# Chunked attention and a gated feed-forward: turning the probabilities by DMA and VectorE instead of TensorE

## The chip, the cores and the metric

The kernel runs on one core of a Trainium2 chip. The metric is the device time of one execution in microseconds; the median of 3 runs of the kernel before is 509.02 us (508.95 to 509.52). Engines go by the names of the profile: PE (TensorE, the matrix products), PEld (its weight loads), DVE (VectorE), ACT (ScalarE), POOL (GpSimd), SP (SyncE, which here only issues DMA transfers). SBUF is the memory of 128 partitions that the engines work in; PSUM, in banks of 128 x 512 float32, takes PE's results.

## The reference

Inputs are q, k, v of 8 batches x 8 heads x 576 rows x 64, all float32, and the weights of the feed-forward. Attention is local to chunks of 64 rows:

```python
q_c = q.reshape(B, H, nc, chunk, D)            # chunk = 64, nc = 9; k_c, v_c alike
scores = scale * np.matmul(q_c, k_c.transpose(0, 1, 2, 4, 3))
scores = scores - np.max(scores, axis=-1, keepdims=True)
attn = np.exp(scores)
attn = attn / (np.sum(attn, axis=-1, keepdims=True) + 1e-09)
out = np.matmul(attn, v_c)
# x = out as (batch, seq, H * D = 512), then the feed-forward, d_ff = 1024:
h = np.maximum(x @ w_in, 0.0)
conv_out = sum over k in 0..2 of conv_w[k] * hp[:, k:k + S, :]   # hp: h padded by one row at both ends
gate = 1.0 / (1.0 + np.exp(-conv_out))
return (h * gate @ w_out).astype(np.float32)
```

## The kernel before

The 4608 rows (8 x 576) are 36 tiles of 128 rows, two chunks each (`t`, two chunks `s`), and 16 units of 288 rows (`u`, half a batch). Attention goes by tiles, the first product of the feed-forward by units, the second by tiles. float32 products of the feed-forward are made of three products of split operands (high and low parts, `x_h`, `x_l`, `wi_h`, `wi_l`, `g_h`, `g_l`, `wo_h`, `wo_l`).

The steps of attention for one tile, with their lines in the profile:

- `load_group`/`load_part` (L134, SP): q and k of three tiles, in pieces of 32 partitions; for tiles below 9 `load_rows` (L114). `load_v` (L146, SP): v of a tile in four DMAs, one for each chunk `s` and each half `hp` of the heads.
- `t_dve` (L163, DVE): q and k turned in blocks of 32 x 32 into `qT` and `kT`; for tiles below 9 `t_pe`/`t_copy` (L154, L158).
- `scores` (L189, PE): 16 products of 64 x 64 into half of two PSUM banks. These are the two banks of `sx`, or, from tile 12 on, also two of the six other banks, which are lent (`lent`, `give_up`) for that from then on.
- `s_max` (L199), `s_sub` (L204), both DVE and reading PSUM; `s_exp` (L209, ACT, tile `e`); `s_sum` (L213), `s_eps` (L216), `s_rec` (L219), DVE, tile `z`; `s_norm` (L222, POOL): e times 1/z.
- `p_pe` (L229, PE): four transposes of 128 x 128 by a product with the identity, into a bank; `p_copy` (L234, ACT): that bank into `pT`.
- `attn_v` (L241, PE): 16 products into half of two banks; `x_hi` (L271, ACT) and `x_lo` (L275, DVE) split the result into `x_h` and `x_l`.

From tile 12 on two tiles go together: one step `both` runs `attn_v` of the last pair and then `scores` of the next pair on PE. A lent bank pair was two tiles of one bank each, so that `s_max` and `s_sub` of a tile that stands there are two instructions (128 x 256 each); on `sx` they are one (128 x 512).

The feed-forward: `mm1` (L284, PE, 12 products of 128 x 290 for each unit and each eighth `f` of d_ff), `h_relu` (L290), `c_mid` (L295), `c_left` (L299), `c_right` (L305), `c_sig` (L311), `c_mul` (L314, which frees the bank), `g_hi` (L324, ACT), `g_lo` (L328, POOL); `mm2` (L337, PE, 3 products of 128 x 512 for each tile and `f`), `o_copy` (L342, ACT), `o_store` (L345, SP). At the start the weights are unpacked and split in ten pieces (L370 to L420, on ACT, DVE and POOL).

What sets the order: all of this is first written down as 2244 steps, each with an engine, a cost, what it comes after and which buffers it takes and frees. A list of numbers, `order_`, gives the order in which a planner places them; it keeps the times of engines and buffers with the steps' costs, and the kernel issues the steps in order of their planned begins. Each engine then runs its own instructions in exactly that order. Up to a planned time of 110 us PE gets warm-up products (L828, fillers) where the plan has it idle.

```python
pe_free = begin[i] + steps[i]["cost"]
steps[i]["fn"](*steps[i]["args"])
```

Buffers that matter here: `e` 3, `z` 2, `pT` 2, `v` 4, and `wt` 4 tiles of 128 x 1024 float32, used by the weights at the start and by `o_copy`/`o_store` later.

Of the kernel before, what the change touches and what calls it, by code (L numbers as in the profile page):

```python
# [30 lines left out]
def attn_ffn(ctx: ExitStack, tc: tile.TileContext, q, k, v, w_in, conv_w, w_out, out):  # L31
# [10 lines left out]
    HS = S // 2  # L42
    XU = HS + 2
# [4 lines left out]
    NU = 2 * B  # L48
# [4 lines left out]
    PAIR = 12  # L53
    scale = 1.0 / float(D) ** 0.5
# [25 lines left out]
    banks = [ps_b.tile([P, 512], F32, name=f"b{i}_ps") for i in range(6)]  # L80
# [57 lines left out]
    def load_v(st, t):  # L138

        r = rawv.tile([P, G, 2, D], F32, name="v")  # L140
        st["v"] = r
        for s in range(2):
            b, t0 = chunk(2 * t + s)
            for hp in range(2):
                j0 = 64 * (hp ^ s)
                nc.sync.dma_start(out=r[j0:j0 + C, :, s, :], in_=v[b, hp::2, t0:t0 + C, :].rearrange("g j d -> j g d"))  # L146
# [18 lines left out]
    def sx_half(i):  # L165

        cols = slice(G * C * (i % 2), G * C * (i % 2) + G * C)
        if i // 2:
            return [(slice(0, 2), sx[:, :, cols])]
        return [(slice(u, u + 1), banks[lent["y", u]].rearrange("p (u n) -> p u n", u=1)[:, :, cols]) for u in range(2)]  # L170

    def sx_bank(i, u):
        parts = sx_half(i)
        return parts[0][1][:, u, :] if len(parts) == 1 else parts[u][1][:, 0, :]
# [7 lines left out]
    def scores(st):  # L182

        qT, kT = st[0], st[1]
        for g in range(G):
            for s in range(2):
                for hp in range(2):
                    d0 = 64 * hp
                    nc.tensor.matmul(  # L189
                        sx_bank(st["s"], hp ^ s)[C * s:C * s + C, C * g:C * g + C],  # L190
# [5 lines left out]
    def s_max(st):  # L196
        st["m"] = work.tile([P, 2, G], F32, name="m")
        for us, sv in sx_half(st["s"]):
            nc.vector.tensor_reduce(out=st["m"][:, us], in_=sv.rearrange("p u (g j) -> p u g j", j=C), op=ALU.max, axis=AX.X)  # L199

    def s_sub(st):
        st["e"] = work3.tile([P, H, C], F32, name="e")
        for us, sv in sx_half(st["s"]):
            nc.vector.tensor_tensor(  # L204
                out=st["e"].rearrange("p (g u) j -> p u g j", u=2)[:, us], in0=sv.rearrange("p u (g j) -> p u g j", j=C),
                in1=st["m"][:, us].rearrange("p u (g o) -> p u g o", o=1).broadcast_to([P, us.stop - us.start, G, C]), op=ALU.subtract)

    def s_exp(st):
        nc.scalar.activation(out=st["e"], in_=st["e"], func=AF.Exp, scale=scale)  # L209

    def s_sum(st):
        st["z"] = work.tile([P, H], F32, name="z")
        nc.vector.tensor_reduce(out=st["z"], in_=st["e"], op=ALU.add, axis=AX.X)  # L213
# [4 lines left out]
    def s_rec(st):  # L218
        nc.vector.reciprocal(out=st["z"], in_=st["z"])  # L219

# [15 lines left out]
    def attn_v(st):  # L236
        for g in range(G):
            for s in range(2):
                for hp in range(2):
                    j0 = 64 * (hp ^ s)  # L240
                    nc.tensor.matmul(  # L241
                        sx_bank(st["x"], s)[D * hp:D * hp + D, C * g:C * g + C],
                        lhsT=st["v"][j0:j0 + C, g, s, :],
                        rhs=st["pT"][j0:j0 + C, g, C * s:C * s + C],
# [8 lines left out]

    def x_views(st, t, x):

        xv = [v_.rearrange("p s (g i) -> p g s i", i=C) for _, v_ in sx_half(st.get("x", 2))]
        parts = []
        for s in range(2):
            b, t0 = chunk(2 * t + s)
            for half, lo, hi in ((0, 0, HS + 2), (1, HS - 2, S)):  # L260
                i, j = max(lo, t0), min(hi, t0 + C)
                if i < j:
                    parts.append((s, i - t0, j - i, (2 * b + half) % NX, i - lo))
        if len(xv) == 1 and [p[1:4] for p in parts] == [(0, C, parts[0][3])] * 2:
            _, _, _, u, o = parts[0]
            return [(xv[0], x[:, u, :, o:o + 2 * C].rearrange("p g (s i) -> p g s i", i=C))]
        return [((xv[0][:, :, s] if len(xv) == 1 else xv[s][:, :, 0])[:, :, i:i + n], x[:, u, :, o:o + n]) for s, i, n, u, o in parts]
# [10 lines left out]
    def mm1(st, u, f):  # L278

        h_ps = banks[st["h"]]  # L280
        n = 0
        for wt, xt in ((wi_h, x_h), (wi_h, x_l), (wi_l, x_h)):
            for kt in range(KT):
                nc.tensor.matmul(  # L284
                    h_ps[:, 0:XU], lhsT=wt[:, f // 2, kt, P * (f % 2):P * (f % 2) + P], rhs=xt[:, u % NX, kt, 0:XU],
# [3 lines left out]
    def h_relu(st):  # L289
        nc.scalar.activation(out=banks[st["h"]][:, 0:XU], in_=banks[st["h"]][:, 0:XU], func=AF.Relu)  # L290

    def c_mid(st, u, f):
        st["i0"] = i0 = 2 * (u % 2)
        st["c"] = work7.tile([P, HS], F32, name="c")
        nc.scalar.mul(out=st["c"], in_=banks[st["h"]][:, i0:i0 + HS], mul=cw[:, FT + f:FT + f + 1])  # L295

    def c_left(st, u, f):
        a, i0, c = 1 - u % 2, st["i0"], st["c"]
        nc.vector.scalar_tensor_tensor(  # L299
            out=c[:, a:HS], in0=banks[st["h"]][:, i0 + a - 1:i0 + HS - 1], scalar=cw[:, f:f + 1], in1=c[:, a:HS],  # L300
            op0=ALU.mult, op1=ALU.add)
# [11 lines left out]
    def c_mul(st):  # L313
        nc.vector.scalar_tensor_tensor(  # L314
            out=st["c"], in0=st["c"], scalar=1.0, in1=banks[st["h"]][:, st["i0"]:st["i0"] + HS], op0=ALU.add, op1=ALU.mult)

    def g_views(u, f):
        g0 = HS * u % GR
        n = min(HS, GR - g0)
        return [(slice(s0, s1), slice(o, o + s1 - s0)) for s0, s1, o in ((0, n, g0), (n, HS, 0)) if s0 < s1]  # L320
# [127 lines left out]
    def split(key, t_load, src, hi=None, lo=None, lo_pool=False, half=False):  # L448
# [5 lines left out]
        if small:  # L454
# [23 lines left out]
    def att(t, key, load_key, writes):  # L478

        st = {}  # L480
        if t < NAT:
            r = "wslot" if t in W_ROWS else "slot"
            ld = step("SP", 1.25, load_key, load_rows, (st, t), take=[(r, st)], lag=3.3)
# [12 lines left out]
        ldv = step("SP", 2.65, load_key + 0.05 if t < 5 else key - 8, load_v, (st, t), [before.get("v")], take=["v"], lag=1.66)  # L496
# [21 lines left out]
        before["x"] = [(st_, t_, soft(st_, s, key + 4 * n) + [v_], w_) for n, (st_, t_, _, v_, w_, _) in enumerate(new)]  # L518
# [15 lines left out]
    def soft(st, s, key):  # L534
        s = step("DVE", 0.69, key, s_max, (st,), [s], take=["m"], bank="sx")
        s = step("DVE", 0.68, key, s_sub, (st,), [s], take=["e"], free=["m", ("sx", "s")], bank="sx")
        s = step("ACT", 0.63, key + 8, s_exp, (st,), [s])
# [5 lines left out]
        return [step("ACT", 0.59, key + 12, p_copy, (st,), [s], take=["pT"], free=[("bk", "pt")])]  # L543

# [8 lines left out]
    def group(j):  # L553
        if j not in group_loads:
# [3 lines left out]
            group_loads[j] = [step("SP", 2.05 if j % 3 != 1 else 4.0, key + 0.1 * n, load_part, (j, n % 2, n // 4, n // 2 % 2), [s], lag=1.25)  # L558
# [18 lines left out]
    until = [-(-(HS * u + HS + (0 if u % 2 else 2)) // P) for u in range(NU)]  # L577
# [285 lines left out]
```

## Time and profile before

| | |
|---|---|
| median of 3 runs | 509.02 us (508.95 to 509.52) |
| the profiled execution | 508.6 us, of which the span of the instructions is 506.8 us |
| instructions | 13087 |
| HBM read, written | 36.72 MB, 9.44 MB |
| first product of `mm1`; last product of `mm2` ends | 36.5 us; about 503.1 us |

A page row of a group reads: line, engine, operation, output<-inputs, shapes, xcount, then busy time in us, the mean ns of one, and the idle time of the engine just before them with what ended it. A row of a timeline reads: start in us, duration in us, then the same names. A row of a table by stage gives for each engine its busy time in that stage with the count of instructions, then the granted PE clock, the share of the DMA engines and GB/s. Durations of products on PE overlap, since it is pipelined; what one costs is read from start to start.

### The profile page before, as it was taken

The page shows a single profiled execution, that of the slowest core. Times are in us where ns is not written, and L with a number is a line of the kernel's source. Part 1 is how long each engine was busy: PE and PEld are TensorE (multiplying, and loading weights), DVE is VectorE, ACT ScalarE, POOL GpSimd, SP SyncE. Part 2 cuts the span into 40 slices and gives each one's busy share as a digit, 9 for nine tenths or more (in the row PEclk, how much of TensorE's full clock was granted, in tenths as well). Part 3 has the DMA queues.
Part 4 walks back from the last instruction along what each step waited for, and adds up shares of the span by engine and source line. Part 5 has one row for each costly group of instructions (what it writes and reads, how often), then busy time and mean ns, then how long its engine had stood idle before and what let it go on. Part 6 is the DMA issues. An engine that isn't in the chain of part 4 may idle for free.

```text
span 506.8 us, 13087 instructions
## 1 busy us (share of the span) xinstructions
PE 495.7 (98%) x5079; PEld 444.9 (88%) x5079; DVE 343.1 (68%) x745; ACT 312.2 (62%) x784; POOL 171.4 (34%) x237
## 2 busy tenths in 40 slices
PE   7999988999999999999999999999999999999997
PEld 7889977899888999989889999988988988998885
DVE  3889999688644787776776785767685856574300
ACT  4569986757535766666655766656665656784511
POOL 1543646425421252333240433333314143241600
PEclk9999999999999999999999999999999999999999
DMA  8987864523265453434445442334612040100111
GB/s 193 229 229 179 224 179 89 88 46 61 45 126 124 118 118 61 94 62 85 107 86 110 83 101 46 74 81 76 150 19 63 23 125 2 49 17 0 44 43 62
DMA packets 183171, 47.04 MB, mean 93 GB/s; under 512 B 175404, under 2 KB 175428, under 8 KB 183108
## 3 DMA queue, kind: packets, MB, share of 16 engines
q1 hardware_dynamic: 183108, 46.20, 40.7%
q8 instruction: 40, 0.66, 0.6%
q14 instruction: 23, 0.19, 0.1%
HBM read 36.72 MB, written 9.44 MB: 91 GB/s over the span
## 4 chain that ended last, share of the span: by engine, by line
PE 89%; DVE 5%; ACT 2%; issue 1%; DMA 1%; POOL 0%; SPq 0%; ACTq 0%
PE b_ps L337 39%; PE b_ps L284 38%; PE b_ps L229 3%; PE sx_ps L189 2%; PE sx_ps L241 2%; PE b_ps L241 1%; DMA qk<-in_moe_w_in 1%; PE b_ps L189 1%; PE b_ps L828 1%; DVE wt L379 1%; PE b_ps L154 1%; ACT wt L370 1%; DVE c L314 1%; DVE c L305 1%; DVE c L299 1%
## 5 line engine op out<-in xcount | busy, mean ns | idle before, releaser
L328 POOL TENSOR_TENSOR g_l<-c,g_h 128x288 fp32r<-128x288 f32 (+8 forms) x184 | 112.3, 633 | 204.4 <-ACT g_h L324 181.1
L337 PE MATMUL b_ps<-wo_h,g_h 128*128 128x512 f32 x288 | 116.8, 405 | 0.0
L337 PE MATMUL b_ps<-wo_h,g_l 128*128 128x512 f32 x288 | 113.6, 395 | 0.0
L337 PE MATMUL b_ps<-wo_l,g_h 128*128 128x512 f32 x288 | 113.5, 394 | 0.0
L299 DVE SCALAR_TENSOR_TENSOR c<-b_ps,cw,c 128x287 f32<-128x287 f32 (+1 forms) x128 | 65.4, 511 | 69.6 <-ACT c L295 60.9
L284 PE MATMUL b_ps<-x_h,wi_h 128*128 128x290 f32 x512 | 91.7, 301 | 1.6 <-DVE c L314 1.6
L284 PE MATMUL b_ps<-x_l,wi_h 128*128 128x290 f32 x512 | 89.6, 297 | 0.0
L284 PE MATMUL b_ps<-x_h,wi_l 128*128 128x290 f32 x512 | 89.2, 296 | 0.0
L290 ACT ACTIVATE b_ps<-b_ps 128x290 f32<-128x290 f32 x128 | 50.7, 398 | 60.0 <-PE b_ps L284 56.0
L284 PEld LDWEIGHTS b_ps<-x_h,wi_h 128*128 128x128 f32 x512 | 78.6, 189 | 9.6 <-DVE c L314 2.5
L314 DVE SCALAR_TENSOR_TENSOR c<-c,b_ps 128x288 f32<-128x288 f32 x128 | 57.0, 446 | 31.8 <-ACT c L311 30.9
L311 ACT ACTIVATE c<-c 128x288 f32<-128x288 f32 x128 | 56.3, 442 | 36.0 <-DVE c L305 35.4
L284 PEld LDWEIGHTS b_ps<-x_l,wi_h 128*128 128x128 f32 x512 | 75.9, 190 | 0.0
L284 PEld LDWEIGHTS b_ps<-x_h,wi_l 128*128 128x128 f32 x512 | 75.4, 189 | 0.0
L295 ACT ACTIVATE c<-b_ps,cw 128x288 f32<-128x288 f32 x128 | 63.7, 501 | 8.1 <-POOL g_l L328 0.8
L305 DVE SCALAR_TENSOR_TENSOR c<-b_ps,cw,c 128x288 f32<-128x288 f32 (+1 forms) x128 | 65.4, 512 | 2.7
L222 POOL TENSOR_TENSOR e<-e,z 128x512 f32<-128x512 f32 x36 | 38.5, 1073 | 84.9 <-DVE z L219 64.0
L337 PEld LDWEIGHTS b_ps<-wo_h,g_l 128*128 128x128 f32 x288 | 54.2, 188 | 12.6
L337 PEld LDWEIGHTS b_ps<-wo_h,g_h 128*128 128x128 f32 x288 | 54.4, 189 | 8.7
L324 ACT CAST g_h<-c 128x288 fp32r<-128x288 f32 (+8 forms) x184 | 58.1, 357 | 5.7 <-DVE c L314 5.0
L337 PEld LDWEIGHTS b_ps<-wo_l,g_h 128*128 128x128 f32 x288 | 54.3, 189 | 7.7
L342 ACT ACTIVATE wt<-b_ps 128x512 f32<-128x512 f32 x36 | 21.4, 596 | 25.2 <-PE b_ps L337 25.0
(59 smaller groups left out, 492.6 us busy)
## 6 DMA issues: line engine op xcount, KB each, us to landing
v<-in_v SPq DMA_DIRECT2D x144, 64.0 KB, 2.4
out<-wt SPq DMA_DIRECT2D x36, 256.0 KB, 2.3
qk<-in_q SPq DMA_DIRECT2D x96, 48.0 KB, 2.2
qk<-in_k SPq DMA_DIRECT2D x96, 48.0 KB, 2.2
qk<-in_moe_w_out SPq DMA_DIRECT2D x4, 1024.0 KB, 6.4
qk<-in_k SPq DMA_DIRECT2D x96, 24.0 KB, 1.9
qk<-in_q SPq DMA_DIRECT2D x96, 24.0 KB, 1.9
qk<-in_moe_w_in SPq DMA_DIRECT2D x4, 512.0 KB, 5.2
```

Source lines behind the costliest of these rows:

```text
L222: nc.gpsimd.tensor_tensor(out=st["e"], in0=st["e"], in1=st["z"].rearrange("p (h o) -> p h o", o=1).broadcast_to([P, H, C]), op=ALU.mult)
L284: nc.tensor.matmul(h_ps[:, 0:XU], lhsT=wt[:, f // 2, kt, P * (f % 2):P * (f % 2) + P], rhs=xt[:, u % NX, kt, 0:XU], start=n == 0, stop=n = ...
L290: nc.scalar.activation(out=banks[st["h"]][:, 0:XU], in_=banks[st["h"]][:, 0:XU], func=AF.Relu)
L295: nc.scalar.mul(out=st["c"], in_=banks[st["h"]][:, i0:i0 + HS], mul=cw[:, FT + f:FT + f + 1])
L299: nc.vector.scalar_tensor_tensor(out=c[:, a:HS], in0=banks[st["h"]][:, i0 + a - 1:i0 + HS - 1], scalar=cw[:, f:f + 1], in1=c[:, a:HS], op0 ...
L305: nc.vector.scalar_tensor_tensor(out=c[:, 0:b], in0=banks[st["h"]][:, i0 + 1:i0 + 1 + b], scalar=cw[:, 2 * FT + f:2 * FT + f + 1], in1=c[: ...
L311: nc.scalar.activation(out=st["c"], in_=st["c"], func=AF.Tanh, scale=0.5)
L314: nc.vector.scalar_tensor_tensor(out=st["c"], in0=st["c"], scalar=1.0, in1=banks[st["h"]][:, st["i0"]:st["i0"] + HS], op0=ALU.add, op1=ALU ...
L324: nc.scalar.copy(out=g_h[:, f, gs], in_=st["c"][:, cs])
L328: nc.gpsimd.tensor_tensor(out=g_l[:, f, gs], in0=st["c"][:, cs], in1=g_h[:, f, gs].bitcast(F32), op=ALU.subtract)
L337: nc.tensor.matmul(banks[st["o"]], lhsT=gt[:, f, o:o + P], rhs=wt[:, f, :], start=f == 0 and n == 0, stop=f == FT - 1 and n == 2)
L342: nc.scalar.mul(out=st["os"], in_=banks[st["o"]], mul=0.5)
```

## The change

For tiles 12 and up the probabilities are no longer transposed on PE. `s_exp` writes into one of two `wt` tiles (`of`) that both tiles of a pair share, laid out by halves `b` of the 64 keys. POOL then multiplies by 1/z twice: `s_fold` into the other `wt` tile (`to`), `s_scale` in place in `of`. `p_swap` issues four DMAs of 32 partitions that copy from `of` into `to`: for each group of 32 partitions, the half of the keys whose block belongs to the neighbouring group. `p_dve`, one instruction per tile, turns all 32 x 32 blocks of `to` into `pT`. With that the chunk, not the head half, decides the partitions of `pT`, so v of such a tile is loaded in its natural order, by one DMA (two where a batch ends), and `attn_v` and `scores` take other halves.

The lent banks become one tile `y_ps` of two banks, so `s_max` and `s_sub` are one instruction there too. Some of the planner's costs change, and `order_` is another list, for all tiles, also those below 12. The general form of the units (`UNITS`, `x_window`) gives the same units as before.

Counts over the program, from the two orders: PE transposes of probabilities 144 before, 48 now; ACT copies of them 36 and 12; POOL products with 1/z 36 and 60; DVE turns of probabilities 0 and 24; issues of v 144 and 75; issues of the swap 0 and 48; fillers 158 and 160. The counts of `mm1`, `mm2`, `scores` and `attn_v` products are the same.

The diff, cut to its core:

```diff
+    ONE_PAIR = True
+    TP = 12
...
-    banks = [ps_b.tile([P, 512], F32, name=f"b{i}_ps") for i in range(6)]
+    pair = ps_b.tile([P, 2, 512], F32, name="y_ps")
+    banks = [None] * 6
...
+        if t >= TP:
+            (b0, t0), (b1, t1) = chunk(2 * t), chunk(2 * t + 1)
+            for b, t_, p0, n in [(b0, t0, 0, P)] if b0 == b1 else [(b0, t0, 0, C), (b1, t1, C, C)]:
+                nc.sync.dma_start(out=r[p0:p0 + n].rearrange("p g u d -> p (g u) d"), in_=v[b, :, t_:t_ + n, :].rearrange("h j d -> j h d"))
+            return
...
-        if i // 2:
-            return [(slice(0, 2), sx[:, :, cols])]
-        return [(slice(u, u + 1), banks[lent["y", u]].rearrange("p (u n) -> p u n", u=1)[:, :, cols]) for u in range(2)]
+        return (sx if i // 2 else pair)[:, :, cols]
...
-                        sx_bank(st["s"], hp ^ s)[C * s:C * s + C, C * g:C * g + C],
+                        sx_bank(st["s"], hp if st["t"] >= TP + 2 else hp ^ s)[C * s:C * s + C, C * g:C * g + C],
...
     def s_exp(st):
+        if st["t"] >= TP:
+            nc.scalar.activation(out=two(st, "of").rearrange("p b h j -> p h b j"), in_=st["e"].rearrange("p h (b j) -> p h b j", b=2),
+                                 func=AF.Exp, scale=scale)
+            return
...
+    def two(st, name):
+        if name not in st["two"]:
+            st["two"][name] = work4.tile([P, 2 * DM], F32, name="wt").rearrange("p (n b h j) -> p n b h j", n=2, b=2, h=H)
+        return st["two"][name][:, st["n"]]
+
+    def s_fold(st):
+        z = st["z"].rearrange("p (b h o) -> p b h o", b=1, o=1).broadcast_to([P, 2, H, C // 2])
+        nc.gpsimd.tensor_tensor(out=two(st, "to"), in0=two(st, "of"), in1=z, op=ALU.mult)
+
+    def s_scale(st):
+        z = st["z"].rearrange("p (b h o) -> p b h o", b=1, o=1).broadcast_to([P, 2, H, C // 2])
+        nc.gpsimd.tensor_tensor(out=two(st, "of"), in0=two(st, "of"), in1=z, op=ALU.mult)
+
+    def p_swap(both_):
+        to, of = (both_[n].rearrange("p n b h j -> p n b (h j)") for n in ("to", "of"))
+        for a in range(4):
+            o, i = 32 * a, 32 * (a ^ 1)
+            nc.sync.dma_start(out=to[o:o + 32, :, 1 - a % 2], in_=of[i:i + 32, :, a % 2])
+
+    def p_dve(st):
+        st["pT"] = work.tile([P, G, P], F32, name="pT")
+        nc.vector.transpose(out=st["pT"].rearrange("p g (u b i) -> p b (g u) i", u=2, b=2), in_=two(st, "to"))
...
-                    j0 = 64 * (hp ^ s)
+                    j0, n, m = C * (hp ^ s), s, s
+                    if st["t"] >= TP:
+                        j0, n, m = C * s, hp, hp if st["t"] >= TP + 2 else hp ^ s
...
+        if fold:
+            n = step("POOL", 1.05, key + 9, s_fold, (st,), [s, st["two"].get("fold")], take=["wt"] * first, port=True)
+            st["two"]["fold"] = n
+            return [step("POOL", 1.05, key + 9, s_scale, (st,), [n], free=["z"], port=True)]
...
+        ends = [soft(n[0], s, key + 4 * i)[0] for i, n in enumerate(new)]
+        s = step("SP", 2.5, key + 14, p_swap, (pair_,), ends, free=["wt"], lag=0.9)
+        ends = []
+        for n in new:
+            s = step("DVE", 0.7, key + 16, p_dve, (n[0],), [s], take=["pT"], free=["wt"] if n is new[-1] else [])
+            ends.append([s])
...
     order_ = [
-        0, 33, 12, 82, 101, 34, 35, 36, 13, 14, 15, 37, 16, 38, 1, 17, 40, 39, 83, 85, 84, 86, 120, 88, 87, 2,
+        0, 12, 33, 82, 101, 13, 14, 15, 34, 16, 35, 17, 1, 36, 37, 38, 40, 83, 39, 85, 84, 86, 120, 88, 87, 89,
```

In the rows of the two orders the new program has other line numbers: L384 is `mm2`, L330 `mm1`, L279 `attn_v`, L196 `scores`, L232 `s_rec`, L346, L352 and L361 `c_left`, `c_right` and `c_mul`, L255 `p_dve`, L251 `p_swap`, L139 `load_part`, L392 `o_store`.

First place, PE around a `both` in the long middle of the program. Before:

```order
L229 MATMUL b_ps<-ident,e 128x128 x4
L337 MATMUL b_ps<-wo_h,g_h 128x512
L337 MATMUL b_ps<-wo_l,g_h 128x512
L337 MATMUL b_ps<-wo_h,g_l 128x512
L229 MATMUL b_ps<-ident,e 128x128 x4
L284 MATMUL b_ps<-x_h,wi_h 128x290 x4
L284 MATMUL b_ps<-x_l,wi_h 128x290 x4
L284 MATMUL b_ps<-x_h,wi_l 128x290 x4
L241 MATMUL sx_ps<-pT,v 64x64 x32
L189 MATMUL b_ps<-kT,qT 64x64 x32
```

and after the change, at a `both` of that stage:

```order
L330 MATMUL b_ps<-x_h,wi_h 128x290 x4
L330 MATMUL b_ps<-x_l,wi_h 128x290 x4
L330 MATMUL b_ps<-x_h,wi_l 128x290 x4
L384 MATMUL b_ps<-wo_h,g_h 128x512
L384 MATMUL b_ps<-wo_l,g_h 128x512
L384 MATMUL b_ps<-wo_h,g_l 128x512
L279 MATMUL y_ps<-pT,v 64x64 x32
L196 MATMUL sx_ps<-kT,qT 64x64 x32
```

The two groups of four transposes are gone; only products of the feed-forward stand ahead of `attn_v` and `scores`.

Second place, DVE at the last pair (tiles 34 and 35), from the last reciprocal on. Before:

```order
L219 RECIPROCAL z<-z 128x8
L314 SCALAR_TENSOR_TENSOR c<-c,b_ps 128x288
L299 SCALAR_TENSOR_TENSOR c<-b_ps,cw,c 128x287
L305 SCALAR_TENSOR_TENSOR c<-b_ps,cw,c 128x288
L314 SCALAR_TENSOR_TENSOR c<-c,b_ps 128x288
L299 SCALAR_TENSOR_TENSOR c<-b_ps,cw,c 128x287
L305 SCALAR_TENSOR_TENSOR c<-b_ps,cw,c 128x288
L314 SCALAR_TENSOR_TENSOR c<-c,b_ps 128x288
L275 TENSOR_TENSOR x_l<-b_ps,x_h 128x4x64 x2
```

and after the change:

```order
L232 RECIPROCAL z<-z 128x8
L361 SCALAR_TENSOR_TENSOR c<-c,b_ps 128x288
L346 SCALAR_TENSOR_TENSOR c<-b_ps,cw,c 128x288
L352 SCALAR_TENSOR_TENSOR c<-b_ps,cw,c 128x287
L361 SCALAR_TENSOR_TENSOR c<-c,b_ps 128x288
L346 SCALAR_TENSOR_TENSOR c<-b_ps,cw,c 128x287
L352 SCALAR_TENSOR_TENSOR c<-b_ps,cw,c 128x288
L361 SCALAR_TENSOR_TENSOR c<-c,b_ps 128x288
L346 SCALAR_TENSOR_TENSOR c<-b_ps,cw,c 128x287
L352 SCALAR_TENSOR_TENSOR c<-b_ps,cw,c 128x288
L255 STREAM_TRANSPOSE pT<-wt 128x2x8x32
```

Nine instructions of the feed-forward now stand between the last reciprocal and the first turn of the probabilities, which waits for the DMAs.

Third place, SP's queue (DMA issues) at about two thirds of the program. Before:

```order
L134 DMA qk<-in_q 32x6x32 x16
L134 DMA qk<-in_k 32x6x32 x16
L134 DMA qk<-in_q 32x6x32 x8
L146 DMA v<-in_v 64x4x64 x4
L345 DMA out<-wt 128x512
```

and after the change:

```order
L139 DMA qk<-in_q 32x12x32 x4
L139 DMA qk<-in_q 32x6x32 x8
L251 DMA wt<-wt 32x2x256 x4
L139 DMA qk<-in_k 32x6x32 x8
L392 DMA out<-wt 128x512
```

The four pieces of a swap stand behind twelve parts of q and ahead of eight of k, in a queue that SP issues one after the other.

More of the change, by code (lines that the diff above doesn't have):

```diff
@@ L42, in attn_ffn @@
     HS = S // 2
+    CUTS0 = [0, HS]
     XU = HS + 2
@@ L280, in mm1 @@
         h_ps = banks[st["h"]]
+        lo, hi = x_window(u)
+        st["w"], st["n"] = hi - lo, UNITS[u][1] - UNITS[u][0]
         n = 0
@@ L536, in soft @@
         s = step("DVE", 0.68, key, s_sub, (st,), [s], take=["e"], free=["m", ("sx", "s")], bank="sx")
-        s = step("ACT", 0.63, key + 8, s_exp, (st,), [s])
+        fold = st["t"] >= TP
+        first = fold and not st["n"]
+        s = step("ACT", 0.63, key + 8, s_exp, (st,), [s, fold and st["two"].get("exp")], take=["wt"] * first, free=["e"] * fold)
+        st.get("two", {})["exp"] = s
         s = step("DVE", 0.68, key + 9, s_sum, (st,), [s], take=["z"])
@@ L543, in soft, with soft_all @@
         return [step("ACT", 0.59, key + 12, p_copy, (st,), [s], take=["pT"], free=[("bk", "pt")])]
+    def soft_all(new, s, key):
+        if new[0][1] < TP:
+            return [soft(n[0], s, key + 4 * i) for i, n in enumerate(new)]
+        pair_ = {}
+        for i, n in enumerate(new):
+            n[0].update(two=pair_, n=i)
+        ends = [soft(n[0], s, key + 4 * i)[0] for i, n in enumerate(new)]
[4 more added lines that the diff above has]
+            ends.append([s])
+        return ends
     def x_steps(st, t, s, key, writes):
@@ L614, in attn_ffn @@
             t, begun = begun, begun + 1
-            over = [v_ for v_ in range(NU) if any(HS * v_ - 2 < P * t + P and P * t < HS * v_ + HS + 2 for _ in (0,))]
+            over = [v_ for v_ in range(NU) if x_window(v_)[0] < P * t + P and P * t < x_window(v_)[1]]
             writes = [mm1_of[v_ - NX, f] for v_ in over if v_ >= NX for f in range(FT)]
@@ L821, in attn_ffn @@
                 taken[b][-1][1] = end[i]
+    lent_ = [lent["y", 0], lent["y", 1]]
+    for i in range(6):
+        banks[i] = pair[:, lent_.index(i), :] if i in lent_ else ps_b.tile([P, 512], F32, name=f"b{i}_ps")
     pe_free, until_ = 2.0, 110.0
```

121 lines of the change are left out of this document (65 added, 56 removed), and 241 rows, old and new, of the table order_.

## The prediction

> **What bounds the kernel now.** I read the page's busy table first, then a table by stage, then the chain that ended last, then TensorE's instructions in order of time around one pair of tiles.
>
> ```profile
> PE 495.7 (98%) x5079; PEld 444.9 (88%) x5079; DVE 343.1 (68%) x745; ACT 312.2 (62%) x784; POOL 171.4 (34%) x237
> ```
> ```profile
> core 0: us, PE busy (x) PEld busy (x) DVE busy (x) ACT busy (x) POOL busy (x), PEclk, DMA share, GB/s
> 0.00:83.00 83.00, 75.61 (x989) 68.79 (x989) 69.03 (x127) 59.00 (x120) 37.75 (x33) 1.00 0.79 196
> 83.00:503.10 420.10, 420.10 (x4102) 376.16 (x4092) 274.04 (x619) 252.62 (x663) 133.66 (x205) 1.00 0.34 72
> ```
>
> The second table says it: from 83.0 to 503.1 us PE is busy for 420.10 of 420.10 us at a granted clock of 1.00, while DVE is busy for 65%, ACT for 60%, POOL for 32%. There every microsecond of PE work is a microsecond of time. Tiles 12 and up, the only ones whose probabilities are turned in a new way, all lie in this stage. The first 83 us are another stage: there DVE is busy for 69.0 us and PE partly fills time with warm-up products.
>
> ```profile
> PE 89%; DVE 5%; ACT 2%; issue 1%; DMA 1%; POOL 0%; SPq 0%; ACTq 0%
> PE b_ps L337 39%; PE b_ps L284 38%; PE b_ps L229 3%; PE sx_ps L189 2%; PE sx_ps L241 2%; PE b_ps L241 1%; DMA qk<-in_moe_w_in 1%; PE b_ps L189 1%; PE b_ps L828 1%; DVE wt L379 1%; PE b_ps L154 1%; ACT wt L370 1%; DVE c L314 1%; DVE c L305 1%; DVE c L299 1%
> ```
>
> L229 is p_pe, the transposes of the probabilities. It holds 3% of the chain for 36 tiles; the change takes 24 of the 36 away.
>
> **Removed: PE transposes.** The price of four of them, from starts in PE's own queue:
>
> ```profile
> 160.13 0.60 PE L229 MATMUL b_ps<-ident,e 128*128 128x128 f32 x4
> 160.48 0.48 PE L337 MATMUL b_ps<-wo_h,g_h 128*128 128x512 f32 x1
> 160.80 0.39 PE L337 MATMUL b_ps<-wo_l,g_h 128*128 128x512 f32 x1
> 161.03 0.39 PE L337 MATMUL b_ps<-wo_h,g_l 128*128 128x512 f32 x1
> ...
> 162.66 0.60 PE L229 MATMUL b_ps<-ident,e 128*128 128x128 f32 x4
> 163.02 0.78 PE L284 MATMUL b_ps<-x_h,wi_h 128*128 128x290 f32 x4
> 163.64 0.70 PE L284 MATMUL b_ps<-x_l,wi_h 128*128 128x290 f32 x4
> 164.18 0.70 PE L284 MATMUL b_ps<-x_h,wi_l 128*128 128x290 f32 x4
> ```
> ```profile
> 168.79 1.09 PE b_ps L241 x64
> 169.88 0.93 PE sx_ps L189 x64
> ```
>
> From 160.13 to 160.48 the four take 0.35 us, and the product behind them is followed after 0.32 us instead of 0.23 (160.80 to 161.03): 0.09 for the turn. The other: 0.36, and 0.62 instead of 0.54, so 0.08. Together 0.44 us per tile. 24 tiles x 0.44 = **10.5 us off PE**. Scores (L189) and attn_v (L241) keep their number. Scores still change the half of the rows at each product; attn_v still takes two on one half, then two on the other, shifted by one. So I cost the new layout at nothing. The chain's two rows differ by 0.16 us for 64 records each, which is what such an order can matter: +-0.16 per pair, +-1.9 in all.
>
> **Removed and added beside PE.**
>
> ```profile
> L222 POOL TENSOR_TENSOR e<-e,z 128x512 f32<-128x512 f32 x36 | 38.5, 1073 | 84.9 <-DVE z L219 64.0 <-ACT g_h L324 11.3 <-DVE wt L432 6.7
> L234 ACT COPY pT<-b_ps 128x512 f32<-128x512 f32 x36 | 21.0, 584 | 12.0 <-PE b_ps L229 11.6
> L163 DVE STREAM_TRANSPOSE qT<-qk 128x512 f32<-128x512 f32 x27 | 18.8, 696 | 0.0
> L199 DVE TENSOR_REDUCE m<-sx_ps 128x8 f32<-128x512 f32 x25 | 17.1, 684 | 10.6 <-PE sx_ps L189 10.4
> L199 DVE TENSOR_REDUCE m<-b_ps 128x4 f32<-128x256 f32 x22 | 8.2, 415 | 5.3 <-ACT x_h L271 5.3
> ```
>
> ACT loses 24 copies x 0.584 = 14.0 us. POOL gets two products per tile for one: 24 x 1.073 = +25.8. DVE gets 24 transposes x 0.696 = +16.7, and on 11 tiles one maximum of 0.684 takes the place of two of 0.415, the subtraction alike: 11 x 2 x 0.146 = -3.2. In the stage DVE then has 274.0 + 13.5 = 287.5 us of about 410 (70%), ACT 58%, POOL 39%. None becomes the bound by its sum; these costs lie beside PE work as long as each pair's chain is in time.
>
> **Added wait: the chain of a pair.** Between a pair's scores and its attn_v stood one POOL product per tile, a PE transpose and an ACT copy. Now: two POOL products per tile, four SP transfers for both tiles, a DVE transpose per tile. The transfer does not exist in this trace; the nearest rows are loads of v, four 64-partition pieces of 64 KB, the same size as a piece of the swap:
>
> ```profile
> 167.60 2.58 SPq L146 DMA_DIRECT2D v<-in_v  x4
> 184.80 16.46 SPq L134 DMA_DIRECT2D qk<-in_q  x28
> DMA to landing us min/median/max: 2.3/2.4/7.3
> ```
>
> Four issues take 2.58 us, so the fourth goes out at 1.94 and lands 2.4 later: 4.3 us for the swap, up to 9.2 at the longest landing, 7.3. I take 4.3: past the first stage the rings are a third busy (0.34 above). From the last reciprocal to the first pT transpose a pair needs 2 x 1.073 + 4.3 = 6.5 us. What the new list gives it is DVE work placed between the two:
>
> ```profile
> L299 DVE SCALAR_TENSOR_TENSOR c<-b_ps,cw,c 128x287 f32<-128x287 f32 (+1 forms) x128 | 65.4, 511 | 69.6 <-ACT c L295 60.9
> L314 DVE SCALAR_TENSOR_TENSOR c<-c,b_ps 128x288 f32<-128x288 f32 x128 | 57.0, 446 | 31.8 <-ACT c L311 30.9
> ```
>
> In the last pair (shown ahead) nine of these stand there: 6 x 0.511 + 3 x 0.446 = 4.4 us, and at a DVE load of 70% they spread over 6.3 us: 0.2 short of 6.5. That is the tightest of the twelve; the others, counted alike, have 5 to 8.5 us of work there, 7 to 12 in time. So the list leaves room for 4.3 but not for much more. Where a pair is late, the transposes hold up VectorE's queue: c_left, c_right and c_mul behind them free no bank, and PE's next attn_v, with all behind it, waits. Today's spacing shows what a list not spread out would cost:
>
> ```profile
> 181.85 0.19 DVE L219 RECIPROCAL z<-z 128x8 f32<-128x8 f32 x1
> 183.25 0.19 DVE L219 RECIPROCAL z<-z 128x8 f32<-128x8 f32 x1
> 184.99 1.05 POOL L222 TENSOR_TENSOR e<-e,z 128x512 f32<-128x512 f32 x1
> 189.00 0.59 ACT L234 COPY pT<-b_ps 128x512 f32<-128x512 f32 x1 [0.54 <-PE b_ps L229]
> 190.49 1.16 PE L241 MATMUL sx_ps<-pT,v 64*64 64x64 f32 x64
> ```
>
> From 183.44 to 190.49 lie 7.05 us. The new chain needs two more POOL products (the first tile's second and its own), so its scale ends near 188.2 instead of 186.04, the swap at 192.5, the transposes at 193.8: 3.3 us late. Twelve pairs: 40 us. So the unknown lies between 0 and 40 us. The nearest to the new list is its own spacing, near 0. I take **2.0 us**, for this reason:
>
> ```profile
> 62.61 2.37 POOL L388 TENSOR_TENSOR wo_l<-wt,wo_h 128x1024 fp32r<-128x1024 f32 x1 [0.49 <-ACT wo_h L420]
> ...
> 62.99 2.03 DVE L216 TENSOR_SCALAR z<-z 128x8 f32<-128x8 f32 x1
> ...
> 83.00:503.10 420.10, 7.03 (x29) 1.00 0.34 72
> ```
>
> L216 adds epsilon to 8 numbers, 0.15 us of work. Here it began beside a POOL product and ended as that ended (64.98 and 65.02). In the long stage 29 of them (last row) average 0.24 us, so about 0.09 of waiting each. With twice the POOL products per pair I take 0.17 us per pair: 12 x 0.17 = 2.0. The Trainium skill, "SBUF — State Buffer", on the shared port pair, says that the pair is an exclusive lock held for a whole instruction, the other engine blocking fully. By that rule alone each pair could lose one whole product, 1.07 us, 12.9 in all, and the time would be 511; the row of 62.99 agrees with the lock, the mean of 0.24 with its being rare.
>
> **SP.** 96 v issues become 27 for the 24 tiles, 48 swap issues come: 21 fewer, at 0.6 us each 13 less. v is loaded tiles ahead into four buffers, so that costs nothing; the swap is urgent, and stands between runs of q and k parts (28 in 16.46 us: 0.59 each).
>
> **First stage.** Tiles below 12 keep their work, but the list is new in every row. Fillers stay about the same in number (160 for 158), and the last of the ten weight pieces has about 3 us less DVE work listed ahead of it (68.8 for 72.1 us, its rows at the trace's means). I cost the stage at 0, with -2 to +3.
>
> **Sum.** The profiled execution took 508.6 us, 1.8 more than its span of 506.8; the median of the runs is 509.0, 0.4 above it. 506.8 - 10.5 + 2.0 = 498.3; + 1.8 = 500.1; + 0.4 = **500.5 us**.
>
> **Rivals.**
> - *Nothing is late* and the first stage gains its 2 us: 509.0 - 10.5 - 2 = 496.5. For it: PE waits for nothing in the stage now.
> - *The swap stands behind other transfers on SP* (the other side). Its place is SP's queue, where up to 12 q or k parts stand right ahead of it. If it waits for four parts, 4 x 0.59 = 2.4 us, less some 0.8 us of spare, 1.6 x 12 = 19 us are lost: 509.0 - 10.5 + 19 = 517.5. It decides from 10.5 / 12 = 0.88 us per pair. Against it: the list holds fewer SP issues than before.
> - *The four pieces land one after another:* 4 x 2.4 = 9.6 us instead of 4.3, 5.3 more, less about 2.5 of spare in a middling pair: 2.8 x 12 = 34, so 532. Against it: v's pieces, issued 0.65 us apart, each land 2.4 us after their own issue, so they overlap. The Trainium skill, "DMA: Bandwidth & Descriptors", in its rules for kernel authors, says that transfers to disjoint partition halves serialize and advises one transfer; the landings above speak against a whole landing for each.
> - *The freed time is eaten* by a worse first stage and waits of 0.6 us per pair: 509.0 - 10.5 + 3 + 7.2 = 508.7, no change.
> - *PE's work does not shrink:* excluded by its order, which holds 48 such transposes for 144.
>
> **Chances.** Less than about 0.2% (1 us) this kernel's measurement cannot tell from none. The forecast, with waits of 0 to 4 us and the first stage's small shifts: 497.5 to 504, 0.62. Below: 0.10. Partly eaten, 504 to 508: 0.09. Even, 508 to 510: 0.06. Slower, SP's queue 0.10 and pieces in turn 0.03. Faster 0.81, same 0.06, slower 0.13. The range reaches from 496.5 (0.07 below) to 510 (0.13 above).
>
> **What would show it.** Right: PE again busy for all of the stage, some 410 us long; POOL near 197 us; pT transposes of 0.7 us on DVE with little idle time ahead of them; swap pieces landing in 2.4 us. Wrong: idle time on PE ahead of attn_v in every pair, released by DVE's pT; DVE idle ahead of pT, released by the swap; landings far above 2.4; or a first stage longer than 83 us.

## The result and the profile after

The changed kernel takes 505.34 us (median of 4 runs, 505.31 to 505.49), the kernel before 508.99 (4 runs, 508.5 to 509.52): ratio 0.9929, 95% interval [0.9911, 0.9946]. It is faster by 3.65 us; 8.5 were forecast. The profiled span is 503.3 us.

The busy row, the chain and the table by stage of the changed kernel (the table's columns are those of the prediction's second table; its last row ends where the last product ends):

```profile
PE 488.8 (97%) x4985; PEld 435.8 (87%) x4985; DVE 353.2 (70%) x736; ACT 299.4 (59%) x749; POOL 194.4 (39%) x261
...
PE 85%; DVE 5%; SPq 4%; ACT 3%; issue 1%; DMA 1%; POOL 0%; ACTq 0%; DVEq 0%; POOLq 0%
```
```profile
0.00:83.00 83.00, 76.20 (x948) 68.86 (x952) 64.82 (x122) 57.33 (x113) 33.51 (x30) 1.00 0.81 198
83.00:499.60 416.60, 412.63 (x4051) 366.96 (x4041) 288.42 (x615) 241.46 (x637) 160.92 (x232) 1.00 0.37 80
```

Before, PE was busy for all of the time from 83.0 us on. Now 4.0 us are missing there (416.60 against 412.63), and PE's share of the chain fell from 89% to 85%, with DVE unchanged at 5%, SP's queue at 4% and ACT at 3%. The next table says where it waits: four stretches of an eight-part table.

```profile
40.00:60.00 20.00, 18.12 (x239) 16.32 (x237) 16.20 (x32) 16.67 (x37) 6.58 (x4) 1.00 0.87 217
...
100.00:120.00 20.00, 18.34 (x227) 16.02 (x226) 14.11 (x30) 12.90 (x39) 5.66 (x12) 1.00 0.31 54
120.00:140.00 20.00, 18.09 (x128) 15.18 (x127) 14.64 (x32) 9.63 (x25) 4.44 (x8) 1.00 0.23 41
140.00:480.00 340.00, 339.99 (x3464) 305.12 (x3463) 247.85 (x526) 202.67 (x535) 139.24 (x200) 1.00 0.39 86
```

In the kernel before, the first three of these stretches read:

```profile
40.00:60.00 20.00, 20.00 (x263) 19.30 (x262) 19.35 (x39) 18.99 (x42) 9.05 (x7) 1.00 0.88 221
...
100.00:120.00 20.00, 20.00 (x241) 18.11 (x240) 16.29 (x35) 13.36 (x40) 5.99 (x11) 1.00 0.31 54
120.00:140.00 20.00, 20.00 (x166) 17.00 (x164) 14.89 (x32) 11.61 (x29) 9.68 (x15) 1.00 0.29 50
```

From 140 to 480 us, where all twelve swaps lie, PE loses nothing in the changed kernel. It is idle for 1.9 us between 40 and 60, 1.7 between 100 and 120, 1.9 between 120 and 140, where it had no idle time before. What was lost went before 140 us, and there the new transfers have not begun. PE's list of waits names a tile that the change made, `y_ps`, the two lent banks in one tile:

```profile
PE y_ps L330 <- DVE c L361: 1.4, 2, 0.7
...
PE y_ps L330 <- ACT y_ps L337: 1.1, 1, 1.1
PE y_ps L330 <- ACT c L342: 0.9, 1, 0.9
PE y_ps L330 <- DVE c L352: 0.8, 1, 0.8
PE y_ps L265 <- DVE c L361: 0.7, 1, 0.7
PE y_ps L164 <- ACT pT L270: 0.7, 1, 0.7
```

Each row is: engine, tile and line that waited, what released it, us in total, times, longest. The list has seven rows in which PE waits to write `y_ps`, six of them shown; they add up to 6.0 us. Before they are lent at tile 12, these two banks take `mm1` (L330 now), `mm2` (L384), `t_pe` (L164) and `p_pe` (L265) like any other. One place, from the timelines of PE and DVE:

```profile
121.84 0.40 PE L384 MATMUL b_ps<-wo_h,g_l 128*128 128x512 f32 x1
123.03 0.77 PE L330 MATMUL y_ps<-x_h,wi_h 128*128 128x290 f32 x4 [0.80 <-DVE c L352]
...
124.17 0.69 PE L330 MATMUL y_ps<-x_h,wi_l 128*128 128x290 f32 x4
...
126.68 0.80 PE L330 MATMUL y_ps<-x_h,wi_h 128*128 128x290 f32 x4 [1.11 <-ACT y_ps L337]
```
```profile
121.83 0.51 DVE L346 SCALAR_TENSOR_TENSOR c<-y_ps,cw,c 128x288 f32<-128x288 f32 x1
122.37 0.52 DVE L352 SCALAR_TENSOR_TENSOR c<-y_ps,cw,c 128x287 f32<-128x287 f32 x1
124.98 0.45 DVE L361 SCALAR_TENSOR_TENSOR c<-c,y_ps 128x288 f32<-128x288 f32 x1 [2.09 <-PE y_ps L330]
```

Here L346 is `c_left`, L352 `c_right`, L361 `c_mul` and L337 `h_relu`. The block that `c_left` and `c_right` read at 121.83 and 122.37 keeps its bank until its `c_mul` at 124.98. So the `mm1` that starts at 123.03 must write the other bank of `y_ps`; yet it waited 0.80 us for `c_right` to finish. Then it goes the other way: `c_mul`, on the first bank, waits 2.09 us until that `mm1` has ended in the second. The 126.68 row is the same again: an `mm1` waits 1.11 us for the `h_relu` of a block that still needs its own bank. Two banks in one tile are treated as one, in both directions, though the planner that made the list counts them as two.

### The profile page after: what moved, and what is told of

It reads as the page before. It is cut to its first block, busy times and chain, and to the rows that moved or that the text cites. A ratio compares the mean times of both kernels' runs of the same rounds, so it can differ in the third digit from the quotient of the medians.

```text
span 503.3 us, 12909 instructions
## 1 busy us (share of the span) xinstructions
PE 488.8 (97%) x4985; PEld 435.8 (87%) x4985; DVE 353.2 (70%) x736; ACT 299.4 (59%) x749; POOL 194.4 (39%) x261
## 4 chain that ended last, share of the span: by engine, by line
PE 85%; DVE 5%; SPq 4%; ACT 3%; issue 1%; DMA 1%; POOL 0%; ACTq 0%; DVEq 0%; POOLq 0%
PE b_ps L384 38%; PE b_ps L330 34%; SPq L139 4%; PE y_ps L330 3%; PE sx_ps L196 2%; PE sx_ps L279 2%; PE y_ps L279 1%; PE b_ps L902 1%; PE y_ps L196 1%; DMA qk<-in_moe_w_in 1%; DVE wt L426 1%; DVE c L352 1%; PE b_ps L265 1%; DVE wt L431 1%; PE y_ps L384 1%
## 5 line engine op out<-in xcount | busy, mean ns | idle before, releaser
L384 PE MATMUL b_ps<-wo_h,g_h 128*128 128x512 f32 x280 | 112.4, 402 | 0.6 <-DVE c L361 0.6
L384 PE MATMUL b_ps<-wo_h,g_l 128*128 128x512 f32 x280 | 110.4, 394 | 0.0
L384 PE MATMUL b_ps<-wo_l,g_h 128*128 128x512 f32 x280 | 110.3, 394 | 0.0
L346 DVE SCALAR_TENSOR_TENSOR c<-b_ps,cw,c 128x287 f32<-128x287 f32 (+1 forms) x116 | 59.0, 511 | 43.7 <-ACT c L342 43.6
L330 PE MATMUL b_ps<-x_h,wi_h 128*128 128x290 f32 x464 | 82.1, 299 | 0.4 <-ACT y_ps L337 0.4
L330 PE MATMUL b_ps<-x_l,wi_h 128*128 128x290 f32 x464 | 81.2, 297 | 0.0
L330 PE MATMUL b_ps<-x_h,wi_l 128*128 128x290 f32 x464 | 80.7, 296 | 0.0
L330 PEld LDWEIGHTS b_ps<-x_h,wi_h 128*128 128x128 f32 x464 | 72.0, 189 | 8.4 <-DVE c L361 1.1
L337 ACT ACTIVATE b_ps<-b_ps 128x290 f32<-128x290 f32 x116 | 46.1, 399 | 50.2 <-PE b_ps L330 49.7
L361 DVE SCALAR_TENSOR_TENSOR c<-c,b_ps 128x288 f32<-128x288 f32 x116 | 51.5, 446 | 27.1 <-ACT c L358 26.1
L330 PEld LDWEIGHTS b_ps<-x_l,wi_h 128*128 128x128 f32 x464 | 68.7, 190 | 0.3 <-DVE x_l L319 0.3
L330 PEld LDWEIGHTS b_ps<-x_h,wi_l 128*128 128x128 f32 x464 | 68.3, 189 | 0.0
L371 ACT CAST g_h<-c 128x288 fp32r<-128x288 f32 (+8 forms) x184 | 58.6, 357 | 10.8 <-DVE c L361 8.8
L384 PEld LDWEIGHTS b_ps<-wo_h,g_l 128*128 128x128 f32 x280 | 52.7, 188 | 12.3
L384 PEld LDWEIGHTS b_ps<-wo_h,g_h 128*128 128x128 f32 x280 | 52.8, 189 | 10.1 <-DVE c L361 1.2
L342 ACT ACTIVATE c<-b_ps,cw 128x288 f32<-128x288 f32 x116 | 57.4, 499 | 6.9 <-POOL g_l L375 0.4
L352 DVE SCALAR_TENSOR_TENSOR c<-b_ps,cw,c 128x288 f32<-128x288 f32 (+1 forms) x116 | 58.8, 511 | 2.6
L384 PEld LDWEIGHTS b_ps<-wo_l,g_h 128*128 128x128 f32 x280 | 52.7, 188 | 8.1
L241 POOL TENSOR_TENSOR wt<-wt,z 128x512 f32<-128x512 f32 x24 | 25.0, 1050 | 68.4 <-DMA qk<-in_k 21.7
```

The costliest lines, as they stand in the source:

```text
L241: nc.gpsimd.tensor_tensor(out=two(st, "to"), in0=two(st, "of"), in1=z, op=ALU.mult)
L330: nc.tensor.matmul(h_ps[:, 0:hi - lo], lhsT=wt[:, f // 2, kt, P * (f % 2):P * (f % 2) + P], rhs=xt[:, u % NX, kt, 0:hi - lo], start=n == 0 ...
L337: nc.scalar.activation(out=h, in_=h, func=AF.Relu)
L342: nc.scalar.mul(out=st["c"], in_=banks[st["h"]][:, i0:i0 + st["n"]], mul=cw[:, FT + f:FT + f + 1])
L346: nc.vector.scalar_tensor_tensor(out=c[:, a:n], in0=banks[st["h"]][:, i0 + a - 1:i0 + n - 1], scalar=cw[:, f:f + 1], in1=c[:, a:n], op0=AL ...
L352: nc.vector.scalar_tensor_tensor(out=c[:, 0:b], in0=banks[st["h"]][:, i0 + 1:i0 + 1 + b], scalar=cw[:, 2 * FT + f:2 * FT + f + 1], in1=c[: ...
```

## Experiments

Three theories stood against each other. T1: this coupling cost the missing time. T2: q and k parts come late between 80 and 130 us (SP's queue had grown to 4% of the chain). T3: the new list is simply worse there.

**1. The changed kernel with two lent tiles.**

```diff
-    pair = ps_b.tile([P, 2, 512], F32, name="y_ps")
...
-        banks[i] = pair[:, lent_.index(i), :] if i in lent_ else ps_b.tile([P, 512], F32, name=f"b{i}_ps")
+        banks[i] = ps_b.tile([P, 512], F32, name=f"b{i}_ps")
...
+        for us, sv in sx_half(st["s"]):     # s_max, s_sub: one instruction per bank again
```

> The changed kernel with the two lent banks as two tiles of their own again, as before the change: maxima and subtractions over them are two instructions each again (11 tiles x 2 x 0.146 = 3.2 us more VectorE work), the list of the order is the changed one in every row, and the swap stays. Three theories for the 7 us that the forecast had and the result has not: T1: one tile over two banks makes a user of one bank wait for the users of the other while both still serve as ordinary banks (up to about 130 us); the kernel then comes to 498.5 us (497 to 501). T2: q and k parts land late behind other transfers between 80 and 130 us; it stays at 505 (504 to 507). T3: the new list is worse in the first 130 us by itself; it stays at 505 (504 to 507).

Measured: 497.62 us (5 runs, 497.36 to 499.27), ratio to the kernel before 0.9764 [0.9729, 0.9798]: 7.7 us under the changed kernel by the medians (8.4 by the two ratios, with some 2 us of uncertainty). The four rows of waits on PE that are left, and the same stretches of its table by stage (its profiled run is the slowest of the five):

```profile
PE sx_ps L282 <- ACT wi_h L470: 2.2, 1, 2.2
PE b_ps L904 <- POOL ident masks.py:199: 1.4, 1, 1.4
PE sx_ps L282 <- issue: 1.2, 1, 1.2
PE b_ps L485 <- DVE wt L482: 0.6, 1, 0.6
```
```profile
40.00:60.00 20.00, 20.00 (x236) 19.12 (x237) 19.13 (x37) 18.37 (x39) 8.14 (x5) 1.00 0.81 208
...
100.00:120.00 20.00, 20.00 (x206) 18.59 (x196) 17.18 (x37) 14.38 (x43) 5.96 (x14) 1.00 0.30 53
120.00:140.00 20.00, 20.00 (x191) 16.74 (x191) 12.47 (x28) 11.66 (x27) 9.46 (x14) 1.00 0.31 68
140.00:480.00 340.00, 340.00 (x3402) 305.39 (x3402) 246.71 (x550) 198.78 (x531) 134.00 (x194) 1.00 0.39 84
```

The idle time in these stretches is gone, and none of the four waits left is for a step of the feed-forward that reads a bank. Between 20 and 40 us this run is worse than the changed kernel (3.6 us idle against 1.5, at a granted clock of 0.91), but over the first 140 us PE is idle for 5.7 us here and 10.8 there. Since the list is the same, the same transfer can be timed in both kernels: issues of the swap, first and last start, here and then in the changed kernel (durations in ns ahead of them):

```profile
L254 SPq DMA_DIRECT2D wt<-wt x48: 587/596/1633, 159.7 to 415.9; - x48
```
```profile
L251 SPq DMA_DIRECT2D wt<-wt x48: 586/596/1888, 166.0 to 422.3; - x48
```

The changed kernel is 6.3 us behind at its first swap and 6.4 behind at its last; the two profiled executions differ by 6.0 us in all (505.31 and 499.27), so between these two all of the loss comes ahead of the new work. T1 holds, T2 and T3 fall: list and loads are the same in both kernels.

**2. The kernel before with one lent tile.**

```diff
-    banks = [ps_b.tile([P, 512], F32, name=f"b{i}_ps") for i in range(6)]
+    pair = ps_b.tile([P, 2, 512], F32, name="y_ps")
...
+        banks[i] = pair[:, lent_.index(i), :] if i in lent_ else ps_b.tile([P, 512], F32, name=f"b{i}_ps")
```

> The kernel before with one edit: its two lent banks are one tile of two banks, and maximum and subtraction over them are one instruction each; list, transposes and transfers are those of before. T1 (one tile couples its two banks): 3 to 7 us slower than before, 512 to 516 us, lost before about 130 us, with TensorE waiting on y_ps. T2 and T3: 509 as before, or up to 0.5 us less.

Measured: 513.65 us (513.61 to 513.79), ratio 1.0083 [1.0053, 1.0112], 4.7 us slower than before, with the other list and none of the new transfers. The stages of it:

```profile
0.00:130.00 130.00, 120.23 (x1368) 108.23 (x1369) 102.67 (x196) 89.45 (x199) 55.60 (x60) 1.00 0.64 148
130.00:508.00 378.00, 377.80 (x3713) 337.14 (x3711) 239.67 (x517) 222.00 (x573) 114.94 (x177) 1.00 0.33 72
```

After 130 us PE is busy for all but 0.2 us; the loss again lies ahead, as T1 says. Waits of PE that name `y_ps` add up to 2.2 us here. The coupling costs 4.7 us with the old list and 7.7 with the new; the intervals (2.7 to 5.7 us, and some 6.4 to 10.4) leave it open how much of that difference is due to the list.

**3. The removed PE work put back.** In the kernel with two lent tiles:

```diff
+        for a in tiles:
+            for n in range(4 if a["t"] >= TP else 0):
+                nc.tensor.transpose(out=sx_bank(a["s"], n % 2)[:, P * (n // 2):P * (n // 2) + P], in_=ident, identity=ident)
```

> The kernel with two lent tiles, plus four TensorE transposes of the identity into the scores' half for every tile from 12 on, whose results nobody reads: the work that the change took away, put back without its ACT copy and without any wait. The forecast's price, 0.44 us per four, gives 24 x 0.44 = 10.5 us over the kernel with two tiles: about 509 where that one takes 498.5. If TensorE is not what bounds the long stage, less than 3 us. Without the turn's 0.09 us it is 8.4 us.

Measured: 508.63 us (10 runs, 508.22 to 509.92), ratio 0.9996 [0.9976, 1.0016]; over the 497.62 of experiment 1 that is 11.0 us, 0.46 for each four (by the two ratios 11.8, with some 2 us of uncertainty each way). Their rows, by form:

```profile
L292 PE MATMUL sx_ps<-ident 128*128 128x128 f32 x52 | 7.1, 273 | 0.0
L292 PE MATMUL b_ps<-ident 128*128 128x128 f32 x44 | 6.1, 272 | 0.0
```

The 96 stand in PE's queue without idle time ahead of them. The rise agrees with the forecast's price of the removed work, 10.5 us, and is far from the less than 3 us expected if PE did not bound the long stage.

**4. The swap 2.4 us later.** In the kernel with two lent tiles, four small transfers ahead of each swap:

```diff
+        spare_ = work1.tile([P, 2, 32], F32, name="sp")
+        for a in range(4):
+            o, i = 32 * a, 32 * (a ^ 1)
+            nc.sync.dma_start(out=spare_[o:o + 32], in_=of[i:i + 32, :, a % 2, 0:32])
```

> The kernel with two lent tiles, plus four small transfers (32 x 2 x 32 numbers each into a scratch tile) ahead of the four pieces of each swap on SP's queue, about 0.6 us each: the swap goes out some 2.4 us later in each pair. The forecast's count of the room (0.2 us short in the last pair, some 2.5 us spare in a middling one): the time rises by 2 to 6 us over the kernel with two tiles. If the pairs have no room, 12 x 2.4 = 29 us. If they have more than 2.4 us of room each, less than 1 us.

Measured: 518.49 us (4 runs, 514.84 to 519.75), ratio 1.0162 [1.0115, 1.021]: 20.9 us over experiment 1, 1.74 per pair. Neither 2 to 6 nor the full 29. The four runs scatter: the lowest, which is the profiled one, is 17.2 us over experiment 1 (1.44 per pair) at a granted clock of 0.997, the other three run at 0.987 to 0.990. SP's issues, DVE's wait for the swap, PE's longest wait, and one stretch by stage, first of this kernel, then of the one without delay:

```profile
L255 SPq DMA_DIRECT2D sp<-wt x48: 587/595/1541, 159.6 to 431.7; - x48
L258 SPq DMA_DIRECT2D wt<-wt x48: 585/595/1626, 162.9 to 434.3; - x48
```
```profile
DVE pT L262 <- DMA wt<-wt: 26.9, 10, 4.8
```
```profile
PE b_ps L337 <- ACT wt L396: 5.7, 3, 2.8
```
```profile
140.00:420.00 280.00, 267.37 (x2917) 238.81 (x2916) 207.31 (x467) 156.36 (x412) 106.74 (x148) 1.00 0.47 98
```
```profile
140.00:420.00 280.00, 280.00 (x2999) 251.66 (x2999) 218.29 (x492) 165.34 (x439) 114.38 (x157) 1.00 0.46 97
```

The first swap goes out 3.3 us behind the first added transfer: one longer issue and three of about 0.6. In experiment 1 the first piece of that swap was the longer one, so its last piece is 2.4 us later here. Ten of the twelve pairs then wait for the swap instead of three, and PE loses 12.6 us in 280. By price the list leaves a pair about 1 us of room, not 2.5.

But the pair's own chain is not the only way in which a late swap costs time. Of the 12.6 us PE spends 3.3 ahead of `attn_v`, waiting for the turn, and 3.6 waiting for `c_mul`, of which 2.3 stand right behind a late turn in DVE's queue. The largest part, 5.7 (PE's row above), is `mm1` (L337 in this kernel) waiting for `o_copy` (L396) to free a bank. `o_copy` needs a `wt` tile, and each swap holds two of the four until it has landed: ACT sat idle ahead of `o_copy` for 10.6 us in three places until a swap was done, against 2.0 in two without delay. The forecast did not count this path.

**5. Another pair of banks in one tile.** In the kernel with two lent tiles, two of the four banks that are never lent share a tile; no instruction comes or goes:

```diff
+    free_ = [i for i in range(6) if i not in (lent["y", 0], lent["y", 1])]
+    pair = ps_b.tile([P, 2, 512], F32, name="o_ps")
...
+        banks[i] = pair[:, free_.index(i), :] if i in free_[:2] else ps_b.tile([P, 512], F32, name=f"b{i}_ps")
```

> The kernel with two lent tiles, but two of the four banks that are never lent are one tile of two banks instead. The list is the same, no instruction comes or goes. T1 (a user of one bank of such a tile waits for the users of the other): the pair is an ordinary one for the whole run, not for the first 130 us alone; the changed kernel lost 497.6 to 505.3, 7.7 us, in those 130, so some 497.6 / 130 x 7.7 = 29 us, with 15 to 40 as bounds: 513 to 538, with waits of TensorE on o_ps throughout. If the coupling costs only where the first stage is short of VectorE, about 505; if it was not the coupling but something of the lent banks, 498.

Measured: 560.23 us (559.43 to 561.02), ratio 1.1019 [1.1, 1.1039]: 62.6 us over experiment 1, more than twice the 29 expected and beyond its bound of 40. The waits of PE, and the long stage:

```profile
PE o_ps L333 <- DVE c L364: 11.4, 12, 2.1
PE o_ps L387 <- ACT c L345: 6.3, 9, 2.0
PE o_ps L333 <- DVE c L355: 5.0, 5, 2.0
PE o_ps L387 <- DVE c L364: 3.0, 6, 1.2
PE o_ps L387 <- DVE c L355: 2.7, 3, 1.2
```
```profile
130.00:554.00 424.00, 385.02 (x3605) 325.64 (x3603) 254.75 (x566) 210.41 (x553) 139.33 (x200) 0.99 0.33 72
```

The second row alone decides: `mm2` (L387 in this kernel) waits for `c_mid` (L345). A bank with `mm1`'s product is freed only by `c_mul`, some steps behind `c_mid`, so a wait that ends with `c_mid` is a wait for the other bank of the tile. The direction of T1 is confirmed with nothing else changed; its price per microsecond of run, carried over from the first 130 us, was too low by more than half. Past 130 us, when two of the six banks are lent, four ordinary ones are left; that this is why the same coupling costs more there is argued, not shown.

**6. The swap 0.6 us later**: experiment 4 with one added transfer.

```diff
-        for a in range(4):
+        for a in [0]:
             o, i = 32 * a, 32 * (a ^ 1)
             nc.sync.dma_start(out=spare_[o:o + 32], in_=of[i:i + 32, :, a % 2, 0:32])
```

> The kernel with two lent tiles, plus one small transfer (32 x 2 x 32 numbers into a scratch tile) ahead of the four pieces of each swap: the swap goes out about 0.6 us later. In the trace of the kernel with two tiles three of twelve pairs already wait for the swap (3.5 us in all, without loss on TensorE), the others have 0.3 to 3 us of room; four such transfers cost 20.9 us. Room counted pair by pair gives 0 to 2.4 us more: 497.6 to 500. A loss in proportion to the delay from the first bit on would give 20.9 / 4 = 5.2 us: 503.

Measured: 499.67 us (4 runs, 498.8 to 502.47), ratio 0.984 [0.9801, 0.988]: 2.0 us over experiment 1 by the medians, within the count of room pair by pair and below a loss in proportion (5.2). By the two ratios it is 3.9, with some 2.7 us of uncertainty, so the runs alone do not exclude 5.2. The trace speaks for the count: from 140 to 420 us PE is idle for 0.4 us of 280. Five pairs wait for the swap now:

```profile
DVE pT L262 <- DMA wt<-wt: 7.6, 5, 2.5
```

Of all versions the one of experiment 1 is the fastest: the new way of turning the probabilities, with two lent tiles.

## Why the forecast was half right

**The step that failed is the first stage's, costed at 0 with -2 to +3.** It cost 7.7 us instead. The edit that makes the lent banks one tile was costed by its instructions alone (two maxima and two subtractions become one each, 3.2 us of DVE work that hides). That the two banks serve as ordinary ones up to tile 12, and that a tile is what waits are set by, was not asked. Experiment 1 measures the cost, experiment 2 shows it with the other list, experiment 5 with another pair of banks. The stage itself was also read too short: the loss reaches to about 130 us, past the forecast's edge at 83. The new list, with all the rest of the change, was rightly costed near nothing: experiment 3, which has PE's old amount of work, two lent tiles, the new list and the swap, stands 0.35 us under the kernel before, within the interval of its ratio. That is a sum; what the list costs by itself no run shows.

**PE transposes:** 10.5 forecast, 11.0 measured. The method held: start to start in PE's own queue, with the turn.

**The chain of a pair:** 2.0 forecast, 0 measured (PE is busy for 339.99 of 340 us in the stage of the swaps). The price came from 0.09 us of waiting that `s_eps` was thought to have beside POOL products. In the changed kernel, with 60 products with 1/z on POOL instead of 36, the mean from 83 us on fell from 0.242 us to 0.215:

```profile
L229 DVE TENSOR_SCALAR z<-z 128x8 f32<-128x8 f32 x29 | 6.2, 215 | 0.5
```

So more POOL work did not bring more of these waits, and the 511 us that a whole product lost in each pair would have given did not come. The turns of the probabilities took the 0.7 us forecast and waited for the swap three times, without loss on PE:

```profile
L255 DVE STREAM_TRANSPOSE pT<-wt 128x512 f32<-128x512 f32 x24 | 16.0, 691 | 3.3 <-DMA wt<-wt 3.3
```

**Where the room is:** the forecast held the last pair for the tightest, 0.2 us short. The rows of the changed kernel show the reverse. The first pair waits:

```profile
170.72 1.31 DVE L255 STREAM_TRANSPOSE pT<-wt 128x512 f32<-128x512 f32 x2 [2.17 <-DMA wt<-wt]
```
```profile
420.39 2.52 SPq L251 DMA_DIRECT2D wt<-wt  x4
```
```profile
427.74 0.70 DVE L255 STREAM_TRANSPOSE pT<-wt 128x512 f32<-128x512 f32 x1
```

In the last pair the fourth piece goes out near 422.3 and lands 2.1 us later (row below), at 424.4, and the turn comes at 427.7: 3.3 us of room. Counting DVE's listed work between two steps missed what else DVE waits for on the way: in the last pair DVE is idle for 2.36 us ahead of one `c_left` alone, until ACT's `c_mid` is done.

**The swap:** 2.4 us to land were taken from v's pieces; the page has less.

```profile
wt<-wt SPq DMA_DIRECT2D x48, 64.0 KB, 2.1
```

**The rivals.** *Nothing is late* (496.5) was right for the long stage and wrong for the first 130 us; the kernel of experiment 1, at 497.6, is nearly that case. *Swap behind others on SP* did not come true. Its price, 19 us for 2.4 us of delay less 0.8 of spare, came out near what experiment 4 measured, 17.2 to 20.9, but in part by luck: 5.7 us of PE's loss there came by the `wt` tiles, which that rival did not have. The 2.5 us of spare that the next rival used was too much. The whole gain of 11.0 us would be gone at 11.0 / 12 = 0.92 us per pair; experiment 4 gives 1.74, experiment 6 0.17 (0.32 by the ratios). *Pieces in turn* is excluded: four issues in 2.52 us with 2.1 us to each landing. The Trainium skill, "DMA: Bandwidth & Descriptors", in its rules for kernel authors, says that transfers to disjoint partition halves serialize. The rows here, to four disjoint quarters, show no whole landing for each. *The freed time is eaten* named the right place, a worse first stage, with another cause and under half the size needed (3 for 7.7).

**The terms as measured:** transposes -11.0 (experiment 1 against 3), list, chain and all the rest together -0.35 (experiment 3 against the kernel before), one tile for two banks +7.7 (the changed kernel against experiment 1; 6.4 to 10.4 by the ratios). Being differences of the same four medians they must add up to the result, 508.99 - 11.0 - 0.35 + 7.7 = 505.3; what they tell is the sizes.

The Trainium skill, "PSUM — Partial Sum Buffer", under bank collisions, tells to guard PSUM with semaphores by bank, and that pairs of engines on different banks ran clean. By it the chip asks for none of the waits on the other bank seen here. The trace agrees so far: with two tiles those waits are gone, and the time with them.

## What to carry to other kernels

When buffers are merged into one tile so that one instruction can cover them, cost the tile as one resource in every use it has, also the uses ahead of the place for which it was merged; a list or planner that still counts two will run into waits that its plan does not have. To find such a thing, read PE's waits by tile name, and look whether a reader and a writer that wait for each other are on the same bank at all. Work taken off the bounding engine was worth what it took there, start to start; but each stage has to be searched for what else the diff touches. When a new transfer takes over buffers that another step also uses, count both paths by which its lateness costs time.

## What the runs showed that was not expected

Merging two of four permanently used banks into one tile cost 62.6 us of 497.6, without one instruction more: of all changes measured here the dearest. The same merging of the two lent banks cost 7.7 us with the new list and 4.7 with the old.
